# A gated mixing network on one core: the last channel product in scaled fp16 halves, the gate's remaining tokens in two column groups, a new order

## The chip, the cores and the metric

The kernel runs on one core of one Trainium2 chip. The metric is device time in microseconds of one execution; the median of three runs is compared. The names of the engines are TensorE (PE in the rows; PEld is its weight load), VectorE (DVE), ScalarE (ACT), GpSimd (POOL) and SyncE (SP, which only issues DMAs here).

## The reference

Three blocks follow each other on 4 batches of 576 tokens; sizes are 8 heads of 64, 512 channels, 1024 hidden.

```
attn = softmax(q k^T / 8 + bias(i, j)) v                 # bias from a small relu net on positions
x    = attn as [4, 576, 512]
h    = gelu_tanh(x @ w_in);  u, v = halves of h
v_n  = (v - mean) / sqrt(var + 1e-6) * g_ln               # over the 512 channels of a token
x    = x + (u * (w_sg @ v_n + b_sg)) @ w_out
theta = x @ w_theta
y    = w_tok_r @ (x cos theta) + w_tok_i @ (x sin theta)   # w_tok mixes tokens
u    = x + y
out  = u + relu(u @ w_ch)
```

The weights of the second and third block come as 64-bit numbers and are turned into 32-bit ones on the chip.

## The kernel before

The kernel is written as a recording: each call of an engine is noted with its operands and a sort key, and at the end a planner (`plan`) simulates all engines with a cost per operation (`cost`) and emits every engine's instructions in the order in which they started there. The keys are shifted by the table `SHIFT` (by name of the tile or group), and where two engines could do an operation the tables `BIAS` and the load terms choose. So all the numbers of these tables set the order.

Products of high precision are made of halves: a 32-bit operand is split into a high half (rounded on ScalarE by `split` or `split16`) and a low half (the rest, on VectorE or GpSimd), and `mm3` multiplies high by high, high by low and low by high. `split16` makes fp16 halves and needs a scale, a power of two per operand, so that the halves fit fp16; `split` on fp32r tiles needs none. The scale comes from the sum of squares: ScalarE sums along the free direction, TensorE multiplies by ones, and VectorE turns the total into a power of two with seven integer instructions on one column (`scale_of`).

The stages, with the names in the rows:

- About 0 to 100 us: the position bias (`hq`, `pb`, `bs`).
- About 30 to 515 us: 144 attention tiles (`s`, `e`, `p`, transposed by DMA to `pT`, then `px`), with the gate network of the batch before in between: `v_unit` (tiles `vp`, `gtv`), `u_unit` (`up`, `gtu`), `s_unit` (`sp`, `gg`). A unit takes 128 of 576 tokens; the fifth takes the remaining 64, on 64 partitions.
- About 515 to 640 us: the gate of batch 3, the product with w_out (`s2`, tile `op`), scales (`x_scale`) and the first `theta` (tile `tp`, then sines and cosines in `z`).
- About 640 us to the end: per batch `ymix` (tile `yp`, 216 matmuls of 288 columns on fp16 halves), `theta` of the next batch, and `s4` (tile `cp`, 96 matmuls of 288 columns on fp32r halves `sp_u` and `wc`, then relu, residual and the DMA to `out`).

`yp`, `cp` and `op` share two PSUM buffers (`tag="w", bufs=2`). A block of `cp` ends with one instruction on VectorE:

```
nc.vector.scalar_tensor_tensor(o..., ps[:, :, :SH], 0.0, self.x1[b][:, db]..., op0=ALU.max, op1=ALU.add)
self.ld(self.out[ds, b * S:(b + 1) * S], o)
```

Here `o` is one of two buffers, `x1` holds u, and both carry the name `bias` in the rows, since they lie in the bias tiles' memory.

Of the kernel before, what the change touches and what calls it, by code (L numbers as in the profile page):

```python
# [231 lines left out]
def covers(a, b):  # L232
# [4 lines left out]
    ("bias", "scalar"): 143.8494, ("bias", "sync"): 88.6203, ("biasr", "scalar"): 197.1322,  # L237
    ("biasr", "sync"): 537.8955, ("bs", "scalar"): -21.4279, ("bs", "vector"): -15.5213,
    ("bsg", "scalar"): -489.4486, ("bsg", "sync"): 256.3559, ("g", "scalar"): -100.5873,
    ("g", "sync"): 126.0728, ("gg", "gpsimd"): -284.0791, ("gg", "scalar"): 416.187, ("gg", "sync"): -343.8609,  # L240
    ("gg", "vector"): 8.6001, ("gr", "scalar"): 102.9182, ("gr", "sync"): 182.7022,
    ("ident", "scalar"): 113.0798, ("ident", "sync"): -277.3655, ("kq", "scalar"): 280.3521,
# [14 lines left out]
}  # L257
SHIFT = {
# [5 lines left out]
    "@w_ch": 725.184, "@w_out": 895.3831, "@w_theta": -316.3514, "@w_tok": 209.201, "@y0": -593.6358,  # L264
# [3 lines left out]
    "fa_v": 1560.667, "fa_wi": -140.7679, "fa_ws": 1256.3781, "fa_x": 314.8794, "fac": 37.52, "fb_k": -29.642,  # L268
    "fb_t": 299.3677, "fb_v": 814.7121, "fb_wi": -253.1845, "fb_ws": -902.3606, "fb_x": 132.429,
    "fc_k": -202.2802, "fc_t": -132.5524, "fc_v": 1087.9065, "fc_wi": -1342.3479, "fc_ws": 1014.8274,  # L270
    "fc_x": -556.5921, "fd_v": -487.3747, "fd_wi": -142.9535, "fd_ws": 590.4839, "fs_k": 108.5734,
    "fs_t": -130.3477, "fs_v": 705.2032, "fs_wi": 1688.4624, "fs_ws": 1226.8647, "fs_x": 428.1539,
    "g": 1255.751, "gg": 165.5572, "ghs": -73.1639, "gr": 2128.4586, "gsc": -1013.4387, "gts": 813.0012,
    "gtu": 86.6412, "gtv": 165.3272, "halfpi": -2279.8328, "hq": -87.7516, "ident": -879.598, "ih": -237.2307,
# [358 lines left out]
class K:  # L633
# [579 lines left out]
    def x_prep(self, b, pool, u, key, w=S):  # L1213
        self.nc.key = key
        sp = self.sp_tiles(pool, f"{u}{b}")
        for f in range(4):
            self.split(sp[f][:, :, :w], self.x1[b][:, f, :w])
# [267 lines left out]
```

## Time and profile before

| | us |
|---|---|
| median of 3 runs | 831.53 (829.93 to 832.4) |
| profiled execution, its own time | 833.19 |
| its span, first to last instruction | 831.4 |
| TensorE busy | 728.1 |
| VectorE busy | 607.9 |
| ScalarE busy | 507.0 |
| GpSimd busy | 343.6 |

The rows come from the profiled execution. A span's time is counted from its first instruction. Busy time of TensorE is the time in which some matmul was under way, so it may be busy and yet not at its full rate.

### The profile page before, as it was taken

How to read it: one execution, taken by the hardware profiler on the slowest of the kernel's cores; microseconds unless marked ns; L12 is line 12 of the kernel's file. 1: busy time of each engine (PE TensorE's matmuls, PEld its weight loads, DVE VectorE, ACT ScalarE, POOL GpSimd, SP SyncE). 2: the span in 40 equal slices, each digit the busy share in tenths (PEclk: the TensorE clock that was granted, in tenths of full speed). 3: DMA queues.
4: the chain of work that ended last, by engine and by line, in shares of the span. 5: the costliest groups of instructions: out<-in, count | busy, mean ns of one | idle time of the engine just before them, and what ended most of it. 6: DMA issues, size and time to landing. Idle time of an engine off the chain costs nothing.

```text
span 831.4 us, 17445 instructions
## 1 busy us (share of the span) xinstructions
PE 728.1 (88%) x6490; PEld 465.0 (56%) x6490; DVE 607.9 (73%) x1453; ACT 507.0 (61%) x953; POOL 343.6 (41%) x274
## 2 busy tenths in 40 slices
PE   5787368579889998989889988999889999999998
PEld 2233235256455554644545545776656677677887
DVE  6896388887887587975997989898988844572422
ACT  6896477666787676867747774565466642560500
POOL 0011334434666664756615662354246541360400
PEclk9998657578999998999978999999999999999999
DMA  6777959789998999889789777554452221030101
GB/s 196 193 181 155 261 133 216 166 160 190 188 188 191 169 205 182 160 180 213 195 212 199 157 157 203 172 157 164 117 120 54 40 53 56 1 80 29 44 15 58
DMA packets 221429, 120.78 MB, mean 145 GB/s; under 512 B 195360, under 2 KB 195744, under 8 KB 221344
## 3 DMA queue, kind: packets, MB, share of 16 engines
q1 hardware_dynamic: 211936, 98.86, 55.5%
q10 hardware_dynamic: 9408, 20.81, 7.9%
q8 instruction: 51, 0.84, 0.4%
q14 instruction: 34, 0.28, 0.1%
HBM read 47.68 MB, written 14.16 MB: 74 GB/s over the span
## 4 chain that ended last, share of the span: by engine, by line
PE 38%; DVE 15%; DMA 6%; issue 6%; ACT 3%; POOL 2%; ACTq 0%; DVEq 0%; POOLq 0%; SPq 0%
PE yp L417 11%; PE cp L417 6%; PE s L417 5%; DMA pT<-p 5%; PE sp L417 4%; PE px L417 3%; PE tp L417 3%; DVE bias L417 3%; PE up L417 3%; PE vp L417 2%; DVE e L417 2%; PE op L417 1%; DVE biasr L417 1%; DVE sp_g L417 1%; DVE gg L417 1%
## 5 line engine op out<-in xcount | busy, mean ns | idle before, releaser
L417 POOL TENSOR_TENSOR p<-e,p 128x576 f16<-128x576 f32 x144 | 190.3, 1332 | 240.8 <-ACT p L417 213.4
L417 PE MATMUL s<-kq 64*128 64x288 f32 (+1 forms) x640 | 153.3, 482 | 34.0 <-DVE m L417 32.3
L417 ACT ACTIVATE e<-e,m 128x576 f32<-128x576 f32 x144 | 110.5, 767 | 71.8 <-DVE m L417 51.9
L417 PEld LDWEIGHTS <-pT 128*128 128x128 f16 (+1 forms) x2240 | 84.2, 108 | 69.2 <-DMA pT<-p 32.5
L417 DVE CUSTOM_DVE_ANT_0 e<-s,bias 128x576 f32<-128x576 f32 x128 | 95.5, 750 | 35.8 <-PE s L417 29.9
L417 PE MATMUL px<-v,pT 128*128 128x64 f16 (+1 forms) x2240 | 95.5, 203 | 23.3 <-DMA pT<-p 19.2
L417 PEld LDWEIGHTS s<-kq 64*128 64x128 f32 (+1 forms) x640 | 70.5, 194 | 80.5 <-DVE m L417 46.7
L417 ACT ACTIVATE p<-e 128x576 f16<-128x576 f32 x144 | 94.7, 673 | 8.2 <-DMA pT<-p 3.3
L417 PEld LDWEIGHTS <-z 128*128 128x128 f16 x864 | 84.1, 98 | 25.5 <-ACT z L417 2.3
L417 PE MATMUL yp<-bias,z 128*128 128x288 f16 x576 | 76.5, 286 | 1.6 <-ACT z L417 1.6
L417 PE MATMUL pb<-hq,w2s 128*32 128x288 f32 x576 | 52.8, 430 | 17.1 <-ACT bs L417 8.1
L417 PE MATMUL op<-sp_g,wo 128*128 128x288 f32 x384 | 58.1, 307 | 7.6 <-ACT sp_g L417 2.8
L417 PE MATMUL vp<-wi,xT 128*128 128x512 f16 (+1 forms) x240 | 63.1, 400 | 0.7 <-DVE gg L417 0.5
L417 PEld LDWEIGHTS op<-sp_g,wo 128*128 128x128 f32 x384 | 53.6, 194 | 13.0 <-ACT sp_g L417 3.8
L417 PE MATMUL up<-xT,wi 128*128 128x64 f16 (+1 forms) x384 | 57.8, 290 | 0.0
L417 PE MATMUL sp<-ws,n 128*128 128x64 f16 (+1 forms) x384 | 56.9, 286 | 0.9 <-DVE gtu L417 0.7
L417 PE MATMUL cp<-sp_u,wc 128*128 128x288 f32 x384 | 54.0, 300 | 0.2 <-DVE bias L417 0.2
L417 PEld LDWEIGHTS cp<-sp_u,wc 128*128 128x128 f32 x384 | 51.8, 188 | 1.2 <-DVE bias L417 0.4
L417 DVE TENSOR_SCALAR hq<-lt,nl 128x576 f32<-128x576 f32 x96 | 45.7, 544 | 4.2 <-PE pb L417 2.3
L417 PEld LDWEIGHTS pb<-hq,w2s 128*32 128x32 f32 x576 | 20.8, 112 | 47.4 <-ACT bs L417 17.9
L417 PE MATMUL tp<-wt,xh 128*128 128x512 f16 x192 | 44.7, 380 | 1.9 <-DVE xh L417 1.9
L417 DVE SCALAR_TENSOR_TENSOR bias<-yp,iy,bias 128x576 f32<-128x576 f32 x16 | 13.0, 814 | 41.6 <-PE yp L417 41.5
(222 smaller groups left out, 1222.2 us busy)
## 6 DMA issues: line engine op xcount, KB each, us to landing
bias<-bs SPq DMA_DIRECT2D x32, 288.0 KB
kq<-kq SPq DMA_DIRECT2D x10, 576.0 KB
gr<-dg SPq DMA_DIRECT2D x15, 288.0 KB
out<-bias SPq DMA_DIRECT2D x15, 288.0 KB
xx<-dx SPq DMA_DIRECT2D x14, 288.0 KB
raw<-vp ACTq DMA_DIRECT2D x11, 320.0 KB
kq<-kq ACTq DMA_DIRECT2D x6, 576.0 KB
bias<-w_tok SPq DMA_DIRECT2D x6, 576.0 KB
```

The lines of the kernel that those rows point to most:

```text
L417: getattr(getattr(self.nc, name), m)(*[res(x) for x in a], **out)
```

## The change

Three things change. First, `s4` works on fp16 halves: w_ch is split by `split16` with a scale of its own (`ssq["w_ch"]`, four more sums of squares on ScalarE), u by `split16` with a power of two from a bound on u, which `x_scale` makes ahead from the scale of x and the sum of squares of w_tok (`ck`, a second call of the new `pow_of`). The block's end becomes a relu with the inverse scale on ScalarE and an addition on VectorE or GpSimd. Second, `v_unit` for the remaining 64 tokens computes the 512 channels in two halves of 256 on the two halves of the partitions, with small copies that bring statistics and results together. Third, the one-column tiles move into one tile `small`, and all numbers of the planner's tables are new, as is the cost of a matmul with 64 output rows.

```diff
 BIAS = {
-    ("bias", "scalar"): 143.8494, ("bias", "sync"): 88.6203, ("biasr", "scalar"): 197.1322,
+    ("bias", "scalar"): 80.259, ("bias", "sync"): 144.0582, ("biasr", "scalar"): 178.0047,
...
@@ cost
-        return (n * 0.65 if rhs.shape[0] == 64 else n / 4 if out.shape[0] == 32 else n), rhs.shape[0] / P
+        return (n * 0.65 if rhs.shape[0] == 64 else n * out.shape[0] / P if out.shape[0] in (32, 64) else n), rhs.shape[0] / P
@@ v_unit
+        n = 512 if t < 4 else 256
         for cc in range(4):
             for i, (s, w) in enumerate(((0, 0), (0, 1), (1, 0))):
-                nc.tensor.matmul(ps[:m], self.xt_tok(b, cc, s, t), self.wi[:, w, cc, 512:DFF],
-                                 start=(cc == 0 and i == 0), stop=(cc == 3 and i == 2))
-        v = self.gelu(ps[:m], m, 512, f"v{b}_{t}", 1)
+                for h in range(P // m):
+                    nc.tensor.matmul(ps[h * m:h * m + m, :n], self.xt_tok(b, cc, s, t),
+                                     self.wi[:, w, cc, 512 + h * n:512 + h * n + n],
+                                     start=(cc == 0 and i == 0), stop=(cc == 3 and i == 2))
+        v = self.gelu(ps[:, :n], P, n, f"v{b}_{t}", 1)
...
+        nc.vector.bn_stats(st[:, :6], v)
+        if t == 4:
+            nc.vector.tensor_copy(st[:m, 6:], st[m:, :6])
+        nc.vector.bn_aggr(mv[:m], st[:m, :6 * (P // m)])
...
+        if t == 4:
+            nc.vector.tensor_copy(mv[m:], mv[:m])
+        nc.vector.tensor_scalar(v, v, mv[:, 0:1], mv[:, 1:2], op0=ALU.subtract, op1=ALU.mult)
...
-            nc.scalar.copy(nr[0:64], v)
-            nc.vector.tensor_tensor(nr[64:P], v, nr[0:64], op=ALU.subtract)
+            h = c.tile([P, 256], F16, tag="nh", name=f"nh{b}")
+            nc.scalar.copy(h[m:], v[m:])
+            nc.scalar.copy(nr[:m, :n], v[:m])
+            nc.vector.tensor_copy(nr[:m, n:], h[m:])
+            nc.vector.tensor_tensor(nr[m:, n:], v[m:], h[m:], op=ALU.subtract)
+            nc.vector.tensor_tensor(nr[m:, :n], v[:m], nr[:m, :n], op=ALU.subtract)
@@ x_scale
-        s, v = self.scale_of(self.ssx[b], f"x{b}")
+        s, v, t = self.scale_of(self.ssx[b], f"x{b}")
+        nc.vector.tensor_tensor(t, t, self.ck, op=ALU.mult)
+        u, w = self.pow_of(t, f"u{b}")
+        self.su[b] = u, w
@@ s4
-        sp = self.x_prep(b, self.p_sp2, "u", key - 10)
+        su, iu = self.su[b]
+        for f in range(4):
+            x = self.p_sp2.tile([P, 2, S], F16, tag=f"uh{f}", name=f"uh{f}_{b}")
+            self.split16(x, self.x1[b][:, f], su)
+            sp.append(x)
+        ic = self.col("ic")
+        nc.vector.tensor_tensor(ic, iu, self.ic, op=ALU.mult)
...
-            nc.vector.scalar_tensor_tensor(o.rearrange("p (n t) -> p n t", n=2), ps[:, :, :SH], 0.0,
-                                           self.x1[b][:, db].rearrange("p (n t) -> p n t", n=2),
-                                           op0=ALU.max, op1=ALU.add)
+            nc.scalar.activation(o.rearrange("p (n t) -> p n t", n=2), ps[:, :, :SH], AF.Relu, scale=ic)
+            self.tt(("vector", "gpsimd"), o, o, self.x1[b][:, db], ALU.add)
@@ build
-        self.wc = self.p_s2.tile([P, 2, 4, DM], F32R, tag="wo", name="wc")
+        self.wc = self.p_s2.tile([P, 2, 4, DM], F16, name="wc")
+        sc, self.ic, _ = self.scale_of(self.ssq["w_ch"], "c")
         for i in range(4):
-            self.put_w(self.wc[:, :, i], rc[i], t + 12 + 3 * i)
+            self.put_w(self.wc[:, :, i], rc[i], t + 12 + 3 * i, sc)
```

Three places show what stands where. The first is TensorE at the gate of batch 3, the unit of the remaining tokens (`vp_4`): before, and then after the change.

```order
L417 LDWEIGHTS xT_0_5620
L417 MATMUL vp_4_7440<-wi,xT_0_5620 64x512
L417 LDWEIGHTS xT_0_5620
L417 MATMUL vp_4_7440<-wi,xT_0_5620 64x512
L417 LDWEIGHTS xT_0_5620
L417 MATMUL vp_4_7440<-wi,xT_0_5620 64x512
```

```order
L415 LDWEIGHTS xT_0_5642
L415 MATMUL vp_4_7464<-wi,xT_0_5642 64x256
L415 LDWEIGHTS xT_0_5642
L415 MATMUL vp_4_7464<-wi,xT_0_5642 64x256
L415 LDWEIGHTS xT_0_5642
L415 MATMUL vp_4_7464<-wi,xT_0_5642 64x256
```

Of each pair of matmuls one now goes to PSUM partitions 0 to 63 and one to 64 to 127, each with its weight load; 24 stand where 12 stood.

The second is VectorE at the scale of x of batch 2, which `theta` of this batch needs (`fs_x`, `fa_x` to `fc_x` and after the change `small` are one-column tiles; `mg`, `sn` and `iy` are the factors made of them): before, and then after.

```order
L417 TENSOR_REDUCE fs_x_135<-pk_x_8332 128x1
L417 TENSOR_SCALAR fa_x_134<-fs_x_135 128x1
L417 TENSOR_SCALAR fa_x_134<-fa_x_134 128x1 x2
L417 TENSOR_SCALAR fc_x_132<-fa_x_134 128x1
L417 TENSOR_SCALAR fb_x_133<-fa_x_134 128x1
L417 TENSOR_SCALAR fc_x_132<-fc_x_132 128x1
L417 TENSOR_SCALAR fb_x_133<-fb_x_133 128x1
L417 TENSOR_TENSOR rk_4_8272<-xa_4_8274,rr_4_8270 64x512
L417 TENSOR_SCALAR sn_129<-fc_x_132,fc_t 128x1
L417 TENSOR_TENSOR iy_131<-fc_x_132,fc_k 128x1
```

```order
L415 TENSOR_REDUCE small<-pk_x_8404 128x1
L415 TENSOR_SCALAR small<-small 128x1
L415 TENSOR_TENSOR small<-small 128x1
L415 TENSOR_SCALAR small<-small 128x1 x3
L415 TENSOR_TENSOR rk_4_8297<-xa_4_8299,rk_4_8297 64x512
L415 TENSOR_SCALAR small<-small 128x1 x8
L415 TENSOR_TENSOR small<-small 128x1
L415 COPY mgr_8430<-small 64x1
L415 COPY snr_8463<-small 64x1
L415 TENSOR_SCALAR small<-small 128x1 x2
L415 TENSOR_TENSOR rk_4_8297<-xa_4_8299,rr_4_8295 64x512
```

The one-column instructions of the two powers of two stand interleaved, with the wide ones (`rk`) between them.

The third is the end of VectorE's program, where the last `yp` blocks become u, are split and the last four output blocks are finished: before, and then after.

```order
L417 SCALAR_TENSOR_TENSOR bias_75<-yp_3_10273,iy_123,bias_75 128x576
L417 TENSOR_TENSOR sp_u_10211<-bias_75,sp_u_10211 128x576
L417 SCALAR_TENSOR_TENSOR bias_78<-cp_0_10331,bias_75 128x576
L417 SCALAR_TENSOR_TENSOR bias_78<-cp_1_10389,bias_75 128x576
L417 SCALAR_TENSOR_TENSOR bias_78<-cp_2_10418,bias_75 128x576
L417 SCALAR_TENSOR_TENSOR bias_78<-cp_3_10444,bias_75 128x576
```

```order
L415 SCALAR_TENSOR_TENSOR bias_75<-yp_2_10313,small,bias_75 128x576
L415 SCALAR_TENSOR_TENSOR uh_3_10302<-bias_75,small,uh_3_10302 128x576
L415 SCALAR_TENSOR_TENSOR bias_75<-yp_3_10375,small,bias_75 128x576
L415 SCALAR_TENSOR_TENSOR uh_3_10310<-bias_75,small,uh_3_10310 128x576
L415 TENSOR_TENSOR bias_78<-bias_78,bias_75 128x576 x4
```

VectorE no longer reads `cp` from PSUM; its four additions read what ScalarE wrote. ScalarE's program, which ended with four splits, now ends with the four relu steps:

```order
L415 ACTIVATE uh_3_10310<-bias_75,small 128x576
L415 ACTIVATE bias_78<-cp_0_10433,small 128x576
L415 ACTIVATE bias_78<-cp_1_10491,small 128x576
L415 ACTIVATE bias_78<-cp_2_10522,small 128x576
L415 ACTIVATE bias_78<-cp_3_10547,small 128x576
```

All sixteen additions stand on VectorE, none on GpSimd.

## Rows read from the trace of the kernel before

**Rows 1.** Profile page: the span, then busy us (share of the span) and instructions.
```profile
span 831.4 us, 17445 instructions
...
PE 728.1 (88%) x6490; PEld 465.0 (56%) x6490; DVE 607.9 (73%) x1453; ACT 507.0 (61%) x953; POOL 343.6 (41%) x274
```

**Rows 2.** Stretch: length; busy us (instructions) of PE, PEld, DVE, ACT, POOL; PEclk, DMA share, GB/s.
```profile
240.00:400.00 160.00, 149.87 (x1563) 83.42 (x1562) 119.28 (x360) 118.01 (x240) 99.67 (x84) 0.97 0.95 188
400.00:520.00 120.00, 104.65 (x1116) 59.57 (x1113) 107.69 (x281) 76.17 (x150) 58.80 (x48) 0.91 0.82 188
520.00:580.00 60.00, 58.77 (x367) 41.59 (x366) 52.08 (x99) 32.83 (x62) 24.25 (x19) 0.97 0.52 167
580.00:637.00 57.00, 48.59 (x350) 35.26 (x349) 51.45 (x90) 36.40 (x65) 26.95 (x19) 1.00 0.38 99
637.00:828.00 191.00, 188.28 (x1389) 149.09 (x1387) 90.83 (x120) 71.92 (x116) 59.24 (x46) 1.00 0.16 42
```

**Rows 3.** Chain that ended last, from 645 us: start us, us, what.
```profile
794.99 19.86 PE yp L417 x162
814.86 12.80 PE cp L417 x96
```

**Rows 4.** Timeline of the end: start us, us, engine, line, operation.
```profile
814.89 0.82 DVE L417 SCALAR_TENSOR_TENSOR bias<-yp,iy,bias 128x576 f32<-128x576 f32 x1 [4.29 <-PE yp L417]
815.74 0.69 ACT L417 ACTIVATE sp_u<-bias 128x576 fp32r<-128x576 f32 x1 [5.93 <-DVE bias L417]
816.46 0.76 DVE L417 TENSOR_TENSOR sp_u<-bias,sp_u 128x576 fp32r<-128x576 f32 x1 [0.75 <-ACT sp_u L417]
...
827.68 0.76 DVE L417 SCALAR_TENSOR_TENSOR bias<-cp,bias 128x576 f32<-128x576 f32 x1 [2.44 <-PE cp L417]
```

**Rows 5.** Instructions by form: busy us, mean ns of one, idle before.
```profile
L417 ACT ACTIVATE rk<-tp,mg 128x512 f32<-128x512 f32 x16 | 10.8, 673 | 3.1 <-POOL z L417 2.7 <-PE cp L417 0.4
...
L417 ACT ACTIVATE bs<-pb,cb,rp 128x576 f32<-128x576 f32 x13 | 10.7, 823 | 3.9 <-DMA bias<-bs 2.3 <-PE pb L417 1.6
...
L417 DVE TENSOR_TENSOR wc<-bias,wc 128x512 fp32r<-128x512 f32 x4 | 4.5, 1162 | 0.5 <-ACT wc L417 0.5
...
L417 DVE SCALAR_TENSOR_TENSOR wt<-bias,s2p,wt 128x512 f16<-128x512 f32 x3 | 2.2, 745 | 0.0
```

**Rows 6.** TensorE: two timeline rows, the tile vp (min/median/max ns), two forms.
```profile
48.91 6.63 PE L417 MATMUL pb<-hq,w2s 128*32 128x288 f32 x64 [0.25 <-ACT bs L417]
...
523.88 3.84 PE L417 MATMUL vp<-wi,xT 128*128 128x512 f16 x17
...
L417 PE MATMUL vp<-wi,xT x240: 377/379/634, 201.1 to 535.5; 128*128 128x512 f16 x96, 128*64 128x512 f16 x24
...
L417 PE MATMUL pb<-hq,w2s 128*32 128x288 f32 x576 | 52.8, 430 | 17.1 <-ACT bs L417 8.1 <-ACT hq L417 4.1 <-DVE bs L417 2.3
...
L417 PEld LDWEIGHTS <-xT 128*64 128x64 f16 x48 | 4.5, 109 | 5.2 <-issue 2.1
```

**Rows 7.** VectorE by form: the gate's steps on the remaining tokens.
```profile
L417 DVE TENSOR_TENSOR nr<-gtv,nr 64x512 f16<-64x512 f32 x4 | 4.6, 1162 | 0.1
...
L417 DVE SCALAR_TENSOR_TENSOR gtv<-gtv,vp 64x512 f32<-64x512 f32 x6 | 4.0, 665 | 0.0
...
L417 DVE TENSOR_SCALAR gtv<-gtv,mv,nk 64x512 f32<-64x512 f32 x4 | 3.8, 960 | 0.0
...
L417 DVE BATCH_NORM_STATS2 st<-gtv 64x6 f32<-64x512 f32 x4 | 2.7, 676 | 0.0
...
L417 DVE SCALAR_TENSOR_TENSOR gtu<-gtu,up 128x256 f32<-128x256 f32 x6 | 2.5, 415 | 0.6 <-ACT gtu L417 0.6
```

**Rows 8.** VectorE's timeline at the third scale of x, first and last of eight.
```profile
613.64 0.15 DVE L417 TENSOR_REDUCE fs_x<-pk_x 128x1 f32<-128x5 f32 x1
...
614.64 0.14 DVE L417 TENSOR_SCALAR fb_x<-fb_x 128x1 int32<-128x1 int32 x1
```

**Rows 9.** TensorE's timeline at the first token mixing.
```profile
638.25 1.63 PE L417 MATMUL yp<-biasr,z 128*128 128x288 f16 x12
```

More of the change, by code (lines that the diff above doesn't have):

```diff
@@ new lines @@
+    ("bsg", "scalar"): -414.2987, ("bsg", "sync"): 290.7463, ("g", "scalar"): -16.2384, ("g", "sync"): 96.0398,
+    ("gg", "gpsimd"): -289.0145, ("gg", "scalar"): 396.9911, ("gg", "sync"): -318.6367,
+    ("gg", "vector"): 34.1712, ("gr", "scalar"): 16.2846, ("gr", "sync"): 75.5832, ("ident", "scalar"): 251.1,
+    ("ident", "sync"): -352.736, ("kq", "scalar"): 307.6909, ("kq", "sync"): 444.6441, ("m", "gpsimd"): 38.9134,
+    ("m", "vector"): -1.8582, ("n", "gpsimd"): -82.2887, ("n", "scalar"): -269.3202, ("n", "vector"): 4.326,
@@ new lines @@
+    ("oo", "gpsimd"): 50.9547, ("oo", "scalar"): -177.6458, ("oo", "sync"): -97.3123, ("oo", "vector"): 36.1873,
+    ("p", "gpsimd"): 4.0719, ("p", "scalar"): 114.7336, ("p", "vector"): 135.3602, ("raw", "scalar"): -131.6097,
+    ("raw", "sync"): 567.5162, ("raww_ch", "scalar"): 161.302, ("raww_ch", "sync"): -139.2743,
+    ("raww_out", "scalar"): 353.1403, ("raww_out", "sync"): -140.4962, ("raww_theta", "scalar"): 333.1081,
+    ("raww_theta", "sync"): -64.0685, ("raww_tok", "scalar"): -420.4008, ("raww_tok", "sync"): 124.042,
@@ L257 @@
+    ("rawwi", "scalar"): -255.525, ("rawwi", "sync"): 81.3652, ("rq", "scalar"): -42.1583,
[6 rows of a table added]
 }
 SHIFT = {
[5 rows of a table removed]
-    "@w_ch": 725.184, "@w_out": 895.3831, "@w_theta": -316.3514, "@w_tok": 209.201, "@y0": -593.6358,
[3 rows of a table removed]
-    "fa_v": 1560.667, "fa_wi": -140.7679, "fa_ws": 1256.3781, "fa_x": 314.8794, "fac": 37.52, "fb_k": -29.642,
-    "fb_t": 299.3677, "fb_v": 814.7121, "fb_wi": -253.1845, "fb_ws": -902.3606, "fb_x": 132.429,
-    "fc_k": -202.2802, "fc_t": -132.5524, "fc_v": 1087.9065, "fc_wi": -1342.3479, "fc_ws": 1014.8274,
@@ L290 @@
-    "z": -223.7223, "zb": 1431.7686,
-}
-LOADF, LOADK = 9.424364169007852, 9.769672874286008e-139
-BV = -1.2289825808293022
[5 rows of a table added]
+    "@w_ch": 754.3825, "@w_out": 1151.9312, "@w_theta": -404.924, "@w_tok": 564.6049, "@y0": -702.6337,
[3 rows of a table added]
+    "fa_wi": 149.0432, "fa_ws": 1016.0335, "fac": -239.8442, "fb_v": 999.6868, "fb_wi": -209.6575,
+    "fb_ws": -1114.1408, "fc_v": 1165.4496, "fc_wi": -1395.9987, "fc_ws": 1289.3807, "fd_v": -454.2832,
+    "fd_wi": -428.5019, "fd_ws": 453.6815, "fs": 197.316, "fs_v": 691.1672, "fs_wi": 1636.2041,
@@ L294 @@
+    "xq": -58.0159, "xr": 981.1043, "xs": -139.7631, "xt": -388.3654, "xx": -1279.6992, "yp": -1995.673,
+    "z": 131.7192, "zb": 1375.466,
+}
+LOADF, LOADK = 10.721877725100178, 8.908695835792788e-148
+BV = -4.298140403220686
 TABLES = {AF.Exp: 0, AF.Tanh: 0, AF.Gelu_apprx_tanh: 1, AF.Sin: 2}
-SLACK = 0.03843938218358472
+SLACK = 0.0778193655953486
 ENGS = ("tensor", "vector", "scalar", "gpsimd", "sync")
-YIELDN, YIELDK, YIELDT = 4, -486.4443712997648, 16.192287609186206
+YIELDN, YIELDK, YIELDT = 4, -522.2337248340954, 7.286513876485484
@@ L1174, in scale_of, with col, pow_of @@
         nc.tensor.matmul(ps[:, :n], self.ones, ss, start=True, stop=True)
-        t = self.const.tile([P, 1], F32, name=f"fs_{name}")
+        t = self.col("fs")
         nc.vector.tensor_reduce(t, ps[:, :n], mybir.AxisListType.X, ALU.add)
-        a, s, v = (self.const.tile([P, 1], I32, name=f"f{k}_{name}") for k in "abc")
+        return self.pow_of(t, name) + (t,)
+    def col(self, name):
+        self.cols += 1
+        return self.small[:, self.cols - 1:self.cols].named(name)
+    def pow_of(self, t, name):
+        nc = self.nc
+        a, s, v = (self.col("fa").bitcast(I32) for k in "abc")
         nc.vector.tensor_scalar(a, t.bitcast(I32), 23, None, op0=ALU.logical_shift_right)
@@ L1211, in s2 @@
             nc.scalar.activation(j, self.x1[b][:, db], AF.Square, accum_out=ss[:, db:db + 1])
[L1213 to L1217, printed above, removed]
-        return sp
     def x_scale(self, b):
         nc = self.nc
-        s, v = self.scale_of(self.ssx[b], f"x{b}")
-        iy, mg, sn = (self.const.tile([P, 1], F32, name=f"{n}{b}") for n in ("iy", "mg", "sn"))
+        s, v, t = self.scale_of(self.ssx[b], f"x{b}")
+        nc.vector.tensor_tensor(t, t, self.ck, op=ALU.mult)
+        u, w = self.pow_of(t, f"u{b}")
+        self.su[b] = u, w
+        iy, mg, sn = (self.col(n) for n in ("iy", "mg", "sn"))
         nc.vector.tensor_tensor(iy, v, self.ik, op=ALU.mult)
@@ L1340, in build @@
         self.p_c1 = nc.pool("c1p")
-        self.ssq = {"w_tok": self.sums(9, "k"), "w_theta": self.sums(4, "t")}
+        self.small, self.cols = self.const.tile([P, 80], F32, name="small"), 0
+        self.ssq = {"w_tok": self.sums(9, "k"), "w_theta": self.sums(4, "t"), "w_ch": self.sums(4, "c")}
         todo = [("w_out", DM, i) for i in range(4)] + [("w_theta", DM, i) for i in range(4)]
@@ L1378, in build @@
         nc.grp, nc.key = "@w_theta", t + 15
-        self.st, self.it = self.scale_of(self.ssq["w_theta"], "t")
+        self.st, self.it, _ = self.scale_of(self.ssq["w_theta"], "t")
         sp = self.const.tile([P, 1], F32, name="s2p")
@@ L1385, in build @@
         nc.grp, nc.key = "@w_tok", t + 30
-        sk, self.ik = self.scale_of(self.ssq["w_tok"], "k")
+        sk, self.ik, self.ck = self.scale_of(self.ssq["w_tok"], "k")
+        nc.vector.tensor_scalar(self.ck, self.ck, 4.0, 2.0, op0=ALU.mult, op1=ALU.add)
         free = [self.bm[4][:, 2], self.bm[4][:, 3]] + wr["w_tok"][:6] + [self.bm[3][:, 0]]
```

44 lines of the change are left out of this document (17 added, 27 removed), and 48 rows, old and new, of tables (BIAS, SHIFT).

## The prediction

> **What bounds the kernel now.** The profiled execution takes 833.19 us, 831.4 us of it the span and 1.8 us around it [rows 1]; that is 1.7 us above the median of the runs, 831.53 us. Sums below are differences, so I make them against the profiled execution and take them off the median.
>
> I read the page first: TensorE is busy for 88% of the span and VectorE for 73% [rows 1]. Such an average hides the stages, so I cut the span into stretches next [rows 2]. From 637 to 828 us TensorE is busy for 188.3 of 191 us at the full clock while VectorE and ScalarE are below half: this tail (token mixing `yp`, channel product `cp`, the last `tp`) is bound by TensorE alone. From 580 to 637 us TensorE is busy for only 48.6 of 57 us, VectorE for 51.5: there TensorE waits for VectorE's single-file work. Between 400 and 520 us VectorE is at 90% and TensorE at 87%, neither alone the bound. The chain of waits confirms the tail: its last long pieces are TensorE's, block after block [rows 3], with the last output block's step on VectorE behind them [rows 4].
>
> **The channel product.** The chain gives its rate: 96 `cp` matmuls on fp32r operands in 12.80 us, 133.3 ns each; 162 `yp` matmuls of the same 288 columns on fp16 halves in 19.86 us, 122.6 ns each [rows 3]. There are 384 `cp` matmuls, all in the tail, and they become fp16 with weight loads as `yp` has them. 384 x 10.7 ns = 4.1 us, all on the path, since nothing else limits this stretch: **-4.1 us**. The least I can give is nothing, if fp16 with a weight tile read by `cp` ran slower than with `z`; no row suggests it.
>
> **The end of each output block.** Before, one VectorE instruction does relu and residual (0.76 us, the last at 827.68) [rows 4]. Now ScalarE does the relu with a scale, then VectorE adds. For the 15 blocks that are followed by other matmuls this is hidden: a block takes TensorE 24 x 0.123 = 2.9 us, two PSUM buffers alternate, and ScalarE is busy for 72 of 191 us [rows 2], with 16 x 0.75 = 12 us to come. If that cover went, each block would wait about 0.8 us. The last block is not hidden. A ScalarE instruction from PSUM costs 0.673 us at 512 columns with one per-partition operand and 0.823 at 576 with two [rows 5]; I take 0.75. The addition is priced by the 0.76 us difference at 816.46 [rows 4], as much as the instruction it replaces. With a hand-over of 0.05: **+0.8 us**.
>
> In front of the last `cp` block stands a chain from the last `yp`: 814.89 VectorE 0.82, 815.74 ScalarE 0.69, 816.46 VectorE 0.76, so the low half is ready at 817.22 [rows 4]. Both splits now have a scale column; ScalarE's fp16 split and VectorE's may each take 0.1 us more. `cp` reaches this low half after 20 matmuls, now at 814.86 + 20 x 0.1226 = 817.31 us, and it is ready at 817.42: **+0.1 us**.
>
> **The remaining tokens of the gate.** 17 `vp` matmuls of 512 columns take 3.84 us, the shortest of them lasting 0.377 with its latency, so (3.84 - 0.377) / 16 = 0.216 us each in a row [rows 6]. The 64 remaining tokens need 12 of them per batch, 2.6 us, in half of the array's columns. Now there are 24 of 256 columns, alternately for the lower and the upper 64 columns of the array. If the two halves run at once this is 1.3 us; if not, 2.6 as before. The nearest row is the bias product, 64 matmuls of 32 columns of weights in 6.63 us, 104 ns each while one lasts 430 ns: four column groups do overlap [rows 6]. So I take 1.3 us saved per batch, 5.2 us in four. Batches 0 to 2 are spread over the attention, where TensorE is not alone the bound; batch 3 lies in the dense 520 to 580 us, but what it saves there can be lost to VectorE's bound behind it. I count half: **-2.6 us**, bounds 0 and -5.2.
>
> What could take the saving back is the weight load in front of each matmul: 24 of 64 columns, 109 ns each, would be 2.6 us if they lay bare, and the unit 3.9 us. The 17 full-height matmuls above had a load before each and still came every 0.216 us, 512 columns at the full clock, so loads hide under matmuls here [rows 6]. The Trainium skill (TensorE: Matmul & The Clock Gate, Part 3) says otherwise: a weight load overlaps matmuls in flight only where its row group differs, and both halves use all rows. By it the four units would lose 5.2 us where I count a gain of 2.6, and the sum would be +3.3 us.
>
> On VectorE the work for these tokens runs on 128 x 256 in place of 64 x 512. Two gelu steps fall from 0.665 to 0.415 us each [rows 7]; statistics 0.676, normalization 0.96 and the low half 1.162 lose, by the same proportion, about 0.25, 0.4 and nothing (two of half the length); three small copies add 0.5, estimated from the 0.15 us of a one-column step [rows 8]. That is 0.65 us less in each of batches 0 to 2 and 0.15 in batch 3, whose gelu is a single ScalarE step, 2.1 in all, at places where VectorE is 75 to 90% busy [rows 2]: **-1.0 us**, bounds 0 and -2.1. The pow on GpSimd stays; its result now goes through one more copy, hidden behind the other units' matmuls.
>
> **The scales.** Each batch needs a second power of two for `u`, from a bound on its size: one product and seven one-column instructions; w_ch needs its own scale. Between the last attention tile and the first mixing result VectorE's order has 45 instructions more, 303 against 258. Eight such instructions take from 613.64 to 614.78 us, 0.142 us each [rows 8]: 6.4 us. Against it, the four low halves of w_ch cost 1.162 us each; now they are made with a scale, nearest the 0.745 us of w_theta's, and three of them stand behind the first mixing result [rows 5]: 3.9 us less. Net 2.5 us more on an engine that is busy for 90% of 580 to 637 us, where TensorE waits for it: **+2.3 us**, bounds 0 (if the new columns fill VectorE's gaps) and +6.4 (if w_ch was never on the path). ScalarE's four more squares for w_ch cost about 0.7 us each at the price of 512 columns [rows 5], 2.8 us, while ScalarE is at 64% [rows 2]: hidden; without cover, that much.
>
> **The new order.** All constants of the planner changed. Through the position bias the order is the same; afterwards single instructions and DMA queues change places (three more `kq` loads and three gate weights on ScalarE's queue, loads of `xx` on SP's), but units start at almost the same attention tiles. In the tail TensorE begins the mixing only after the other small products, then the same sequence follows. I count 0; bounds are the 9.6 us for which TensorE idles from 520 to 637 us [rows 2], in either direction.
>
> **Sum.** -4.1 + 0.8 + 0.1 - 2.6 - 1.0 + 2.3 = -4.5 us: 828.7 in the terms of the profiled execution, 827.0 us as a median. What a measurement of this kernel can tell from no change is about 0.3%, 2.5 us.
>
> **Rivals.**
> - *All savings land.* Both halves of the column-group saving count fully (-5.2 and -2.1), the one-column work fills gaps (0), and the new order recovers half of the 9.6 us idle: -4.1 + 0.9 - 5.2 - 2.1 - 4.8 = -15.3, 816.2 us. For it: TensorE's idle time before 637 us is mostly wait for VectorE. Against: VectorE has more to do there, not less. Chance 0.22 for anything below 822.
> - *The column groups don't overlap, or the attention hides them.* Then the 24 matmuls take as long as the 12 did, and the total loses 2.6 of its gain: -1.9, 829.6 us, no change that can be told. Against: [rows 6]. Chance 0.16.
> - *The weight loads lie bare.* Two loads of 109 ns stand before each pair of half-length matmuls, and if they wait for the array each unit takes 3.9 us: -4.5 + 2.6 + 5.2 = +3.3, 834.8 us. Against: loads of the same height are hidden in every dense row. Chance 0.03. (This is what the rule of the Trainium skill's page TensorE: Matmul & The Clock Gate, Part 3, would give.)
> - *The one-column chain is the path (the other side).* Place: VectorE from 540 to 637 us. If all 6.4 us delay the first mixing, w_ch's saving is off the path and the attention gives nothing, the tail's 3.2 us don't pay for it: +6.4 - 3.2 = +3.2, 834.7 us. It turns slower than before as soon as more than 3.2 of the 6.4 us count with no gain in front. For it: 90% busy and TensorE waiting; against: half of the columns are ready long before `cp` asks for them, and the order puts most of them between other units' steps. Chance 0.12, in which I include an attention that the new order slows.
> - *The forecast*, 822 to 831 us, 0.47.
>
> The forecast's own range lies partly above 829.0: of its 0.47 I give 0.39 to faster and 0.08 to no change. Faster 0.22 + 0.39 + 0.03 of the second rival = 0.64; same 0.08 + 0.13 = 0.21; slower 0.12 + 0.03 = 0.15. The range leaves out about 0.1 on each side: 817 to 834.5.
>
> **What would show it.** In the changed profile: `cp` in the tail at 122 to 123 ns per matmul; the last piece ScalarE then VectorE, 0.8 us longer; `vp` on 64 rows about 1.3 us per unit; about 6 us more of one-column instructions before the first `yp`; TensorE idle from 580 us to the first mixing 8 to 11 us. If the first `yp` starts more than 3 us later than 638.25 us [rows 9], or TensorE idles in the tail for more than 5 us, the prediction is wrong; likewise if the first `vp` of batch 3, which follows the attention, starts more than 4 us away from 523.9 us [rows 6], since I gave the new order nothing.

## The result and the profile after

The changed kernel takes 819.53 us (median of 4 executions, 814.43 to 824.07) where the kernel before took 831.72 in the same set: ratio 0.9862, 95% interval 0.982 to 0.9905, 12.2 us less. In a second set (below) it was 0.9792 (0.975 to 0.9835). Forecast were 827.0 us and 4.5 us less. The profiled execution is the slowest of the four: 824.07 us, span 822.0. Stretches of it, to be laid beside [rows 2]:

```profile
240.00:400.00 160.00, 148.39 (x1577) 83.82 (x1578) 123.27 (x382) 123.21 (x253) 104.83 (x86) 0.98 0.97 188
400.00:520.00 120.00, 102.09 (x1077) 59.82 (x1078) 105.10 (x263) 69.36 (x137) 51.78 (x42) 0.89 0.80 179
520.00:580.00 60.00, 58.25 (x405) 42.62 (x405) 53.31 (x113) 36.28 (x71) 25.91 (x20) 0.99 0.49 158
580.00:637.00 57.00, 50.08 (x331) 36.30 (x330) 48.29 (x103) 38.01 (x69) 30.16 (x23) 0.94 0.37 97
637.00:822.00 185.00, 179.50 (x1370) 133.58 (x1368) 91.16 (x137) 81.52 (x128) 54.87 (x42) 1.00 0.17 45
```

TensorE is again the only busy engine of the tail (179.5 of 185 us), which is 6 us shorter. In front of it nothing in these rows looks won: 580 to 637 us has 1.5 us more of TensorE. The chain of waits of after (start us, us, what) answers to [rows 3]:

```profile
785.72 20.00 PE yp L415 x162
805.73 11.77 PE cp L415 x96
```

The timeline of after at the first mixing and at the end answers to [rows 9] and [rows 4]:

```profile
634.75 4.26 PE L415 MATMUL tp<-wt,xh 128*128 128x512 f16 x19
...
638.99 0.36 PE L415 MATMUL pk_x<-ss_x,ones 128*128 128x5 f32 x2
639.38 1.63 PE L415 MATMUL yp<-biasr,z 128*128 128x288 f16 x12
...
817.52 0.74 ACT L415 ACTIVATE bias<-cp,small 128x576 f32<-128x576 f32 x1 [2.20 <-PE cp L415]
818.30 0.76 DVE L415 TENSOR_TENSOR bias<-bias,bias 128x576 f32<-128x576 f32 x1 [2.18 <-ACT bias L415]
```

96 `cp` take 11.77 us, 122.6 ns each. Behind the last of them stand ScalarE's relu and VectorE's addition. The first mixing starts 1.1 us later than before, with 24 more theta matmuls done ahead of it (108 of 216; 84 before). The instructions of after by form, to be laid beside [rows 6] and [rows 7]:

```profile
L415 PE MATMUL vp<-wi,xT 128*64 128x256 f16 x96 | 6.9, 276 | 0.0
...
L415 DVE TENSOR_TENSOR nr<-gtv,nr 64x256 f16<-64x256 f32 x4 | 2.5, 629 | 0.3 <-ACT nr L415 0.2
...
L415 DVE SCALAR_TENSOR_TENSOR gtv<-gtv,vp 128x256 f32<-128x256 f32 x6 | 2.4, 408 | 0.0
...
L415 DVE COPY nr<-nh 64x256 f16<-64x256 f16 x4 | 1.9, 465 | 0.1
...
L415 DVE COPY st<-st 64x6 f32<-64x6 f32 x4 | 1.7, 421 | 0.1
...
L415 DVE TENSOR_SCALAR gtv<-gtv,mv 128x256 f32<-128x256 f32 x4 | 1.6, 406 | 0.0
```

TensorE's work for the remaining tokens fell from 12.6 to 6.9 us. VectorE's hardly did: its groups on these tokens sum to 14.4 us against 15.1, since three copies and a second subtraction came in beside the shorter steps.

**Where the time went.** Three points divide each execution: the start of the last `sp` matmul (end of the gate), the start of the first `yp`, and the end. What lies behind the last `sp` came out the same to within half a us wherever the same order was profiled twice (234.5 and 234.1 in two profiles of after, 234.1 in e5 and 234.7 in e9; 240.4 in before, 239.9 in e10); what lies ahead of it differs by up to 11 us between two executions of one program (last section). So I take the parts behind it from the profile, and the part ahead of it as the median less these parts and the 1.8 to 2.1 us around the span:

| | median us (executions) | ratio to before, 95% | last sp to first yp | first yp to end | up to the last sp |
|---|---|---|---|---|---|
| before | 831.72 (4) | | 47.3 | 193.2 | 589.5 |
| after | 819.53 (4) | 0.982 to 0.9905 | 51.9 | 182.6 | 583.0 |
| e1 after again | 819.29 (6) | 0.975 to 0.9835 | 51.5 | 182.6 | 583.1 |
| e2 new code, old tables | 842.22 (12) | 1.005 to 1.0111 | 63.5 | 186.3 | 590.4 |
| e3 old code, new tables | 851.44 (6) | 1.0142 to 1.0211 | 60.9 | 197.1 | 591.6 |
| e4 jitter | 890.77 (6) | 1.0508 to 1.0632 | 71.6 | 201.6 | 615.7 |
| e5 halves apart | 819.77 (6) | 0.9788 to 0.9895 | 51.5 | 182.6 | 583.7 |
| e6 one scale | 816.98 (6) | 0.9724 to 0.985 | 50.6 | 182.6 | 581.9 |
| e7 theta later | 826.86 (12) | 0.9859 to 0.9931 | 50.9 | 190.2 | 583.6 |
| e8 old order, groups | 838.93 (12) | 1.0047 to 1.0111 | 47.1 | 193.4 | 596.7 |
| e9 new, old start | 829.07 (12) | 0.9932 to 0.9997 | 52.0 | 182.6 | 592.3 |
| e10 old, new start | 825.93 (12) | 0.9915 to 0.9987 | 46.6 | 193.2 | 584.3 |
| e11 old, theta earlier | 840.18 (10) | 1.0064 to 1.0146 | 56.9 | 191.8 | 589.7 |
| e12 end in halves | 816.67 (4) | 0.9747 to 0.9869 | 52.4 | 182.3 | 580.0 |

The 12.2 us are therefore 6.5 up to the end of the gate and 5.9 behind it, less 0.3 around the span. The kernel before had medians of 835.97, 833.65 and 830.91 in the sets of e1 to e4, e5 to e8 and e9 to e12; its part up to the last `sp` is then 593.7, 591.4 and 588.7. So times of different sets compare only to some 5 us: against its own set's kernel before, e1 is 16.7 us faster and not 12.2, with 10.7 us of it ahead of the gate's end. The ratios are of executions in the same set and leave out those in a slower state, while the medians are of all executions.

Behind the first `yp` the account closes. TensorE's time by product, from the end of one matmul to the end of the next with idle time taken out, before and after: `cp` 51.6 and 47.3, `tp` 28.6 and 23.7, `yp` 106.6 and 106.2, sums 0.2 and 0, idle 2.4 and 1.0, behind the last matmul 3.8 and 4.5. The differences, -4.3 - 4.9 - 0.4 - 0.2 - 1.4 + 0.7, add up to the measured -10.5. Of that, 4.6 (4.2 in e1) are given back between the last `sp` and the first `yp`.

### The profile page after: what moved, and what is told of

It reads as the page before. It is cut to its first block, busy times and chain, and to the rows that moved or that the text cites. A ratio compares the mean times of both kernels' runs of the same rounds, so it can differ in the third digit from the quotient of the medians.

```text
span 822.0 us, 17628 instructions
## 1 busy us (share of the span) xinstructions
PE 724.0 (88%) x6540; PEld 457.0 (56%) x6540; DVE 606.1 (74%) x1515; ACT 523.0 (64%) x981; POOL 345.6 (42%) x274
## 5 line engine op out<-in xcount | busy, mean ns | idle before, releaser
L415 POOL TENSOR_TENSOR p<-e,p 128x576 f16<-128x576 f32 x144 | 192.8, 1345 | 225.5 <-ACT p L415 192.7
L415 PEld LDWEIGHTS <-pT 128*128 128x128 f16 (+1 forms) x2240 | 86.5, 109 | 74.9 <-issue 38.4
L415 PE MATMUL px<-v,pT 128*128 128x64 f16 (+1 forms) x2240 | 97.7, 204 | 28.8 <-DMA pT<-p 18.1
L415 PE MATMUL op<-sp_g,wo 128*128 128x288 f32 x384 | 61.9, 317 | 8.7 <-DVE bias L415 4.1
L415 PEld LDWEIGHTS op<-sp_g,wo 128*128 128x128 f32 x384 | 56.4, 200 | 13.7 <-issue 4.2
L415 PE MATMUL vp<-wi,xT 128*128 128x512 f16 (+1 forms) x288 | 59.9, 366 | 1.3 <-DVE xT L415 1.2
L415 DVE SCALAR_TENSOR_TENSOR bias<-yp,small,bias 128x576 f32<-128x576 f32 x16 | 13.1, 816 | 50.1 <-PE yp L415 50.1
L415 PE MATMUL cp<-uh,wc 128*128 128x288 f16 x384 | 49.1, 286 | 0.3 <-ACT bias L415 0.3
L415 ACT ACTIVATE bias<-bias 128x512 f32<-128x512 f32 (+1 forms) x34 | 23.0, 677 | 32.9 <-DVE bias L415 21.6
```

Source lines behind the costliest of these rows:

```text
L415: getattr(getattr(self.nc, name), m)(*[res(x) for x in a], **out)
```

## The experiments

The planner makes a new order whenever the code or a table changes. So from e5 on the order is held: the plan is that of the kernel named, and only what is put in a place changes.

**e1, the changed kernel unaltered; e2 and e3, code and tables crossed; e4, the tables jittered.**

```
e2: BIAS, SHIFT, LOADF, LOADK, BV, SLACK, YIELD* of before, in the new code
e3: those of after, in the old code (SHIFT["fs_x"] = SHIFT["fs"], ...)
e4: for k in sorted(SHIFT): SHIFT[k] += uniform(-2, 2)
```

> The changed kernel unaltered, to see how far its executions lie apart and to have a second profile of it. If the gain is a fixed property of the program, the median stays within 2 us of 819.5 and the executions spread as widely as in the first set (814 to 824). If the first set was a chance draw, the median comes nearer to the forecast 827.

> The changed code with the order tables of before (BIAS, SHIFT, LOADF, LOADK, BV, SLACK, YIELD). Theory A (the edits themselves save the 12 us, because all of their savings land): 818 to 822 us. Theory B (the edits save about 4.5 us as summed in the prediction, the refitted order the rest): 826 to 828 us. Theory C (tables fitted to one code are worth less on the other, whatever the edits): above 829 us.

> The code of before with the new order tables (names that the new code merged get the merged name's value). Theory A: 830 to 833 us, as before. Theory B: 823 to 826 us, as the order brings its 7 us without the edits. Theory C: above 834 us.

> The changed kernel with every number of SHIFT moved by a random amount of at most 2 (the numbers reach to some 2000), which reorders only neighbours. If the details of the order are worth little (my bounds for it were plus or minus 9.6 us, taken as 0): within 2 us of the changed kernel. If the refitted order is a narrow optimum that carries a good part of the gain: 4 to 10 us slower than it.

e1 repeats the gain. e2 and e3 are slower than either kernel, so theory C held: code and tables are worth something together only. e2 still has the edit's own mark, `cp` 47.2 us in its tail. e4 lost 71 us: moves of at most 2 in numbers that reach 2000 cost more than four times what the change brought in that set (16.7 us). My bounds for an order, plus or minus 9.6 us, were far too narrow for an arbitrary one. None of the three says which part of the order brought the gain, hence what follows.

**e5, the two halves apart, and e8, the groups alone in the order of before.**

```
e5: -  for cc ...: for i ...: for h in range(2): matmul(half h)
    +  same 24 places: all of half 0, then all of half 1
e8: -  matmul(ps[:64], xt, wi[512:1024])
    +  matmul(ps[0:64, :256], xt, wi[512:768]); matmul(ps[64:128, :256], xt, wi[768:1024])
       (and 128x256 steps with their copies in the places of the 64x512 ones)
```

> The changed kernel, instruction for instruction in its own order on every engine, except that in the places of the 24 matmuls of each vp_4 unit the twelve of the first column half now come first and the twelve of the second half behind them, so that neighbours no longer lie in different column groups. If the overlap of the groups is what halved the matmuls (1.7 us a unit in the trace of after, 3.2 before): the four units take about 12.6 us again instead of 6.9. Theory A (the path through the attention and batch 3's gate feels TensorE): the time before the first token mixing grows by 2.6 (the prediction's half) to 5.7 us. Theory B (hidden): under 1 us. The 182.6 us from the first token mixing to the end stay as they are in both.

> The kernel before, in its own order on every engine, with the two column groups alone: each vp_4 matmul becomes two of 256 columns in two column groups, and the steps behind it take 128x256 tiles, with the copies that the change adds, in the places where the 64x512 ones stood. The prediction's half: 3.6 us faster than before (ratio 0.9957). All of it: 7.3 us (0.9913). Hidden: 0. The 193.2 us from the first token mixing on are unchanged.

The halves' matmuls of e5 by form:

```profile
L420 PE MATMUL vp<-wi,xT 128*64 128x256 f16 x96 | 10.5, 275 | 0.0
```

Apart, the four units take 10.5 us, together 6.9: the column groups do overlap, and neighbours in different groups are what does it. The 12.6 us that I expected are those of the old order, so e5 takes away 3.6 of the 5.7 us that TensorE saved. A cost of these 3.6 us can't be seen: 819.77 against 819.29 us, and the same 51.5 us behind the gate. The two medians are of different sets and the intervals are some 4 us wide to either side, so this alone speaks for theory B without closing the case. e8 points the same way: in the old order the edit brought no gain that can be told. Its interval has it slower by 0.5 to 1.1%; the five executions that the ratio counts have a median of 832.95 us, though, and those of the kernel before 832.56, so a loss is not shown. Behind the gate it takes the same time (240.5 and 240.4 us), TensorE's halves take 7.5 us where the whole matmuls took 12.6, and VectorE's groups on these tokens take 17.9 us where they took 15.1. Whether that VectorE time eats what TensorE saves I did not settle.

**e6, one scale.** The eight one-column instructions of the second scale are left out in each batch.

```
- u, w = self.pow_of(t, f"u{b}")     (no instruction in these eight places)
+ self.split16(x, x1, su -> s); ic = iu -> v * self.ic
```

> The changed kernel in its own order without the second scale: the eight one-column VectorE instructions of it are left out for each batch and the last product is scaled with the scale of x instead (so its scale is not the one that the sum of bounds gives). 32 instructions at 0.142 us are 4.5 us of VectorE. Theory A (the prediction's, they lie partly on the path): 2 to 4.5 us less between the last score tile and the first token mixing. Theory B (VectorE has room there): less than 1 us. From the first token mixing on 182.6 us in both, within 0.3.

VectorE has 4.7 us less of one-column work between the last score tile and the first mixing (15.7 us in e1, 11.0 here), and the first mixing comes 0.8 us sooner behind the gate than in e1 and e5 (50.6 and 51.5; after and e9 have 51.9 and 52.0). So this part of the one-column work costs 0.8 to 1.4 us, a sixth to a third of its length. The median's 2.3 us less lie within the interval.

**e7, theta later, and e11, its mirror in the old order.**

```
e7:  order = head without late + late + rest   (late: 24 matmuls tp1_2, tp1_3 and what hangs on them)
e11: the same 24, with what they need, ahead of the first yp
```

> The changed kernel with 24 theta matmuls of batch 1 (two units, 5.2 us) put behind the 40th matmul of the first token mixing instead of ahead of it; all else keeps its order. Theory A (ahead of the first token mixing they fill TensorE time that waits for z, so that the refitted order won 5.2 us with them): the first mixing starts at the same distance from the last score tile, 143.8 to 145.5 us, within 1 us, and the rest takes 187.8 instead of 182.6 us, the whole 5 us longer. Theory B (they are on the path either way): the first mixing starts 5 us earlier, the rest takes 187.8 us, the whole is unchanged.

> The mirror of the run with theta later: the kernel before in its own order, with the last 24 theta matmuls of batch 1 ahead of the first token mixing. Theory A (worth 5.2 us in any order): from the end of the gate (last sp matmul) to the end of the program 235 instead of 240.4 us. Theory B (free only where TensorE waits for z in front of the first mixing, which it does for under a microsecond in the kernel before): the first mixing comes 5 us later, the rest is 5 to 6.7 us shorter (the 1.57 us wait inside the first mixing is covered), so from the last sp matmul 238.5 to 240.4 us.

TensorE's timeline of e7 at its first mixing:

```profile
631.85 1.25 PE L416 MATMUL tp<-wt,xh 128*128 128x512 f16 x5 [0.86 <-DVE xh L416]
...
635.93 0.59 PE L416 MATMUL pk_x<-ss_x,ones 128*128 128x5 f32 x2 [2.70 <-ACT jx L416]
636.38 3.04 PE L416 MATMUL yp<-biasr,z 128*128 128x288 f16 x12
```

The stretch behind it in e7 (columns as in [rows 2]):

```profile
636.00:642.00 6.00, 6.00 (x29) 4.03 (x30) 5.14 (x37) 4.74 (x8) 2.27 (x2) 0.56 1.10 164
```

TensorE's timeline of e11 at its first mixing:

```profile
636.14 7.03 PE L418 MATMUL tp<-wt,xh 128*128 128x512 f16 x24 [2.60 <-DVE rr L418]
643.00 1.63 PE L418 MATMUL yp<-biasr,z 128*128 128x288 f16 x12
```

Without the 24 matmuls in front, the first `yp` of e7 starts at the same distance from the last score tile (145.3 us; 145.5 in after): it stands behind `pk_x`, which waits 2.70 us for `jx`, the sum of squares of the last x, and not for z as I had it. Then it runs at a granted clock of 0.56, so that 12 `yp` take 3.04 us instead of 1.63. The rest takes 7.6 us longer, 5.2 of theta and 2.4 of `yp`, and the median is 7.6 above e1's: theory A, and dearer than expected. In the old order the same move is a loss, and neither theory's number fits: the matmuls wait 2.60 us for VectorE's `rr`, which reads `tp`, and take 7.03 us, so the first `yp` comes 9.6 us later. The rest is only 1.4 us shorter, since the wait for ScalarE's `z` inside the first mixing, 1.56 us in before, is now 3.13, and `yp` runs 1.8 us longer. From the last `sp` on it takes 248.7 us instead of 240.4. So the gain is not in the move by itself but in its place in the refitted order, where TensorE has a wait ahead of the first mixing to fill: from the last `sp` to the first `yp` it idles 9.4 us in e7 and 5.5 in after.

**e9 and e10, the starts exchanged.** About 1500 operations, to the 18th score tile, take the other tables' order. Laid side by side, the queues of the five engines show 119 lines of difference in e9.

```
+ order = head + [x for x in order if x[0] not in early]   (head: the start under the other tables)
```

> The changed kernel in its own order, save that the operations of its first stretch (about 1500, to the 18th score tile) stand as the old tables put them: 25 rows of TensorE, 46 of VectorE, 41 of ScalarE and 7 of SP's queue differ, among them loads of the gate's weights that go to the other of the two queues. Theory A (the refit of the start brings the time that is won ahead of the gate's end): the tenth score tile comes at 96 instead of 90 us, as it does with the old tables throughout, and the whole takes 825 to 828 us. Theory B (what is won at the start is lost again in the attention): 819 to 821 us. From the first token mixing on 182.6 us in both.

> The mirror: the kernel before in its own order, save that the operations of its first stretch stand as the new tables put them. Theory A: the tenth score tile comes at 91 instead of 97 to 99 us and the whole is 6 to 8 us faster than before (ratio 0.990 to 0.993). Theory B: within 2 us of before. From the first token mixing on 193.2 us in both.

The start decides the part ahead of the gate's end: with the old one the changed kernel goes from 583 to 592.3 us, with the new one the kernel before from 588.7 in that set (593.7 at most) to 584.3. Theory A both times, somewhat above its number in e9 and below it in e10. Within their own set, e12, which differs from after only in its last piece, has 580.0 us (four executions): against it e9 loses 12.3, and e10 wins 4.4 of the 8.7 us between before and e12. So the start is somewhere between half and all of this part. What differs can be seen in the timelines. That of before, ScalarE and the queues that issue (SPq, ACTq), at 84 to 97 us:

```profile
84.53 0.78 ACT L417 ACTIVATE e<-e,m 128x576 f32<-128x576 f32 x1 [1.40 <-POOL p L417]
...
87.53 1.03 SPq L417 DMA_DIRECT2D kq<-kq  x1
88.39 7.25 ACTq L417 DMA_DIRECT2D rawwi<-w_in  x2
...
95.75 0.77 ACT L417 ACTIVATE e<-e,m 128x576 f32<-128x576 f32 x1 [9.06 <-DMA rawwi<-w_in]
```

The same place in after:

```profile
85.47 0.78 ACT L415 ACTIVATE e<-e,m 128x576 f32<-128x576 f32 x1
...
86.25 0.76 ACT L415 ACTIVATE e<-e,m 128x576 f32<-128x576 f32 x1
86.28 0.99 SPq L415 DMA_DIRECT2D kq<-kq  x1
...
87.32 0.99 SPq L415 DMA_DIRECT2D rawwi<-w_in  x2
...
89.20 0.78 ACT L415 ACTIVATE e<-e,m 128x576 f32<-128x576 f32 x1 [0.96 <-DVE m L415]
```

ScalarE's waits from 60 to 100 us in e9 (us in all, times, longest):

```profile
ACT e L418 <- DMA kq<-kq: 6.7, 1, 6.7
```

The waits of the same passes in e10:

```profile
ACT e L420 <- DVE m L420: 2.2, 1, 2.2
```

In before, two loads of the gate's weights (`rawwi`) stand on ScalarE's queue ahead of its passes over the score tiles. The second is issued only at 95.31 us: its record waits for the semaphore that SP's load of `kq` raises, issued at 87.53. ScalarE works in order, so the next pass starts at 95.75, 9.06 us idle. In after the two loads stand on SP's queue behind the same `kq`, where 0.99 us covers them, and ScalarE's passes run through. e9 has the loads on ScalarE again and waits 6.7 us, by its row for `kq`; e10 has no such wait. The tenth score tile comes at 99.3 us in before, 89.8 in after, 95.7 in e9, 91.9 in e10. No other wait of ScalarE from 60 to 100 us differs by so much between the four; these two loads alone I did not move, so that they are the whole of the start's share is not shown. The Trainium skill (DMA: Bandwidth & Descriptors, Issuing engines are not separate DMA queues) says that starting DMAs on several engines only saves the time that issuing takes, which is usually small beside the transfer. Here an issue took 0.33 us, and ScalarE stood still for 9.06 us, 6.6 of them from the end of the first issue (88.72) to the second (95.31).

**e12, the last piece in halves.**

```
- mm3(...); relu 128x576; add 128x576; store
+ 12 matmuls of half 0, 12 of half 1; relu, add, store for each half
```

> The changed kernel in its own order with the very last piece in two halves of 288 columns: all twelve matmuls of the first half, then those of the second, and relu, add and store for each half. In the changed kernel 4.52 us lie behind the last matmul. If ScalarE's relu and VectorE's add of the last piece stand on the path in full (0.75 and 0.76 us): 0.6 to 0.8 us less behind the last matmul, 181.9 instead of 182.6 us from the first mixing. If the store's own 3 us or the second store take it back: 182.5 us or more. The median cannot tell 0.7 us, the trace can.

The timeline of its end:

```profile
815.49 0.89 ACT L420 ACTIVATE bias<-cp,small 128x288 f32<-128x288 f32 x2 [2.20 <-PE cp L420]
816.03 0.85 DVE L420 TENSOR_TENSOR bias<-bias,bias 128x288 f32<-128x288 f32 x2 [1.94 <-ACT bias L420]
...
816.91 0.34 ACTq L420 DMA_DIRECT2D out<-bias  x1
```

4.19 us lie behind the last matmul instead of 4.52: 0.33 us, half of what I expected. ScalarE's first half did not start before 815.49, right behind the last matmul, which starts at 815.17: only that one raises the semaphore that relu waits for, so nothing ran beside the second half's matmuls. It is the shortest version of the tail that I ran, 182.3 us; its median, 816.67 us, can't be told from that of after.

## Why the prediction was right in direction and short in size

The measured 819.53 us lie inside the stated 817 to 834.5 us, but partly by luck: of the 12.2 us, the priced terms below explain 2.5, and the rest came from a term that was put at 0. By number the result belongs to the first rival (below 822 us, chance 0.22), and not by its mechanism: that rival lets the column groups save 5.2 us, where the runs support about 0, and TensorE recover 4.8 us of idle time, where from the last `sp` to the first `yp` it idles 7.5 us before and 5.5 after. Nor can 0.3%, as I wrote, be told from no change: the medians of before in four sets range from 830.91 to 835.97 us.

- **cp, -4.1.** Right: 122.6 ns each, 4.3 us less in the tail, and 47.2 to 47.3 us of it in every order that was run with the new code.
- **The end of a block, +0.8, and the chain before the last cp, +0.1.** The first is right (3.76 to 4.52 us behind the last matmul), the second was nothing: the last `yp` ends at 805.72, `cp` starts at 805.73, and its 96 matmuls take 96 x 122.6 ns, so none of them waits.
- **Column groups, -2.6.** Mis-sized. TensorE saved what I wrote (5.7 us; 5.2 forecast in full), but e5 gives 3.6 us of it back at no cost that can be told, and e8 has it without a gain. Near 0 is what these runs support, the rival "the attention hides them". The rival of bare weight loads fell: in e5, 96 matmuls with a load each take 10.5 us, 109 ns each, where load and matmul one after the other would be about 216. The rule of the Trainium skill (TensorE: Matmul & The Clock Gate, Part 3), that a load overlaps only where row groups differ, does not describe these rows; I had left out the exception for a background weight buffer that the same part makes.
- **VectorE's part, -1.0.** Mis-sized: 0.7 us less VectorE in all, bounds 2.1. I had priced the three copies at 0.5 us. By their means they take 0.42, 0.21 and 0.47 us, but these means mix two cases: in three of their four places each takes 0.17, 0.16 or 0.22 us, 0.55 in all, and in the fourth 1.19, 0.37 or 1.19, beside a GpSimd instruction (last section). My 1.162 us for a low half were such a mean too: two of w_ch's four took 0.69 us and two 1.64.
- **One-column work, +2.3.** 5.3 us more of it stand ahead of the first mixing. e6 prices its larger part at 0.8 to 1.4 us. About 1, within the bounds; the four low halves of w_ch all start behind the first `yp` now (645.48 us and later).
- **The new order, 0.** This is the step that failed, at two places. I had seen that DMA queues change places, listed three gate weights among them, and priced this at nothing; the two `rawwi` loads on ScalarE's queue were a wait of 9.06 us in the trace of before, which I never looked for, as I took the start to be no part of the change. By e9 and e10 the start is half or more of the 6.5 us ahead of the gate's end; what else may lie there (the column groups, VectorE's 0.7 us) no run could tell from nothing. And I wrote that units start at the same tiles and that the mixing's sequence is the same; 24 theta matmuls went ahead of the first mixing, and with the rest of that order they brought about 3.4 us, by subtraction: -5.9 behind the gate, less -4.3, +0.8 and the +1 above. Together these are 9.9 us where my bounds were 9.6, and the bounds came from idle time between 520 and 637 us, where most of it was not.

So -4.3 + 0.8 + 0 + 1 - 6.5 - 3.4 + 0.3 (around the span) = -12.1, the measured difference but for rounding. This closes because -6.5 and -3.4 are what is left over, in the first set; in the second set the part ahead of the gate's end is 10.7. The marks that I named for the order would not have shown the failure: the first `yp` moved 1.1 us, the tail idled 1.0 us, and batch 3's first `vp`, at 510.9 us before, came at 507.9 (the 523.9 that I named was a later run of it, misread). All of them lay behind the start, and in e1, the same program, the first `yp` came at 627.9 and that `vp` at 498.0, so such a mark says little of one execution. Idle time of TensorE from 580 us to the first mixing came out at 7.0 us, below the 8 to 11 that I named.

## What to carry to other kernels

When an edit comes with a new order, read the whole trace of before for engines that stand still behind a load which they issue themselves, and price the order by these waits; the edited stage is not the only place where it acts. To price an edit, hold the order and change what is put in its places: code and tables crossed ran 6.3 and 15.5 us slower than the kernel before, losses that belong to neither. TensorE time saved in a stretch that another engine or a wait bounds can be worth nothing at the end, as the 3.6 us of e5 were as far as could be told, however well the trace shows the saving.

## What the runs showed of the hardware that I had not expected

The profiled executions of after and e1 are of one program. From the first `yp` on they take 182.62 and 182.63 us; ahead of it they differ by 11.5. Stretches of the attention in after (columns as in [rows 2]):

```profile
170.00:180.00 10.00, 9.66 (x81) 5.98 (x78) 6.82 (x26) 4.19 (x9) 5.07 (x4) 0.50 1.16 222
180.00:190.00 10.00, 10.00 (x83) 5.85 (x84) 7.36 (x26) 5.86 (x13) 3.81 (x3) 0.66 0.42 131
200.00:210.00 10.00, 9.51 (x60) 5.24 (x60) 6.26 (x17) 3.02 (x7) 0.82 (x1) 0.50 0.50 139
```

The same stretches in e1:

```profile
170.00:180.00 10.00, 8.22 (x111) 5.07 (x111) 7.98 (x35) 6.17 (x14) 4.74 (x4) 1.00 1.13 234
180.00:190.00 10.00, 7.58 (x67) 4.58 (x67) 8.35 (x21) 5.89 (x14) 5.90 (x5) 0.88 0.85 188
200.00:210.00 10.00, 10.00 (x105) 5.62 (x103) 8.45 (x29) 9.94 (x23) 6.56 (x6) 1.00 1.01 221
```

In after the granted clock is at its lower level (0.50, 1.2 GHz) from 170 to 180 and from 200 to 210 us, in e1 at the upper one; from 160 to 210 us TensorE runs 441 matmuls in the one and 516 in the other. Just ahead, from 160 to 170 us, it was busy for 7.93 us in after and for 8.72 in e1, at nearly the same clock (0.84 and 0.81). The 55th score tile then comes at 231.7 and at 222.2 us. The order of instructions is the same, so the two executions can part only in how long things run and wait. I read it so that some waiting at that point decided at which clock the next stretch ran, and that this spreads the executions; e7's first mixing at 0.56 behind a wait of 2.70 us looks the same in little. That the clock is the cause and not itself the consequence of something else I have not shown by a run, and of the other executions there is no trace.

In these runs VectorE's time depends on what GpSimd does. Here is a copy of two columns on 64 partitions in e1, and behind it what GpSimd does at that time:

```profile
345.71 4.37 DVE L415 COPY mv<-mv 64x2 f32<-64x2 f32 x1
```

GpSimd:

```profile
345.19 2.51 POOL L415 TENSOR_TENSOR p<-e,p 128x576 f16<-128x576 f32 x2
347.67 1.15 POOL L415 TENSOR_TENSOR n<-gtv,n 128x512 f16<-128x512 f32 x1
348.78 1.27 POOL L415 TENSOR_TENSOR p<-e,p 128x576 f16<-128x576 f32 x1
```

The copy, 0.16 us long in three of its four places, starts while GpSimd is at work, lasts 4.37 us through four GpSimd instructions in a row, and ends at 350.08 us, just behind the last of them (350.05). In after the same copy takes 0.37 us and ends at 355.24, where GpSimd's instruction ends at 355.22. The copy `st` of batch 3 shows it again (540.60 to 541.78 us beside GpSimd's `xs`, 540.48 to 541.75). Not all instructions are held so: VectorE's score steps (`e<-s`, which read PSUM) have the same median, within 6 ns, whether a GpSimd instruction is under way at their start or not (750 to 757 ns in before, after and e1). So a mean over a group of VectorE instructions can mix two lengths, and it is worth reading the shortest and the longest before a price is taken from it.
